# A decode kernel of gated attention and MLP: the MLP's hidden units laid out as 10 full groups, 16 and 80 instead of 9 full groups, 64 and 160

## The chip, the cores and the metric

The kernel runs on one core of one Trainium2 chip. The metric is the device time of one execution in microseconds. One execution reads 78 MB from HBM and writes 1 KB.

## The reference

One token of width 512. Attention has 32 heads of 128 with a cache of 4096 positions per head; the MLP has 1376 hidden units and a squared ReLU. A sigmoid gate mixes the two. All inputs are bf16.

```
x = A_x                                              # 1 x 1 x 512
g = sigmoid((x * gate_w).sum(-1))
q = (x @ wq) as 32 heads of 128
p = softmax(q . k_cache / sqrt(128))                 # 32 x 4096
a = (p @ v_cache) as 4096 @ wo                       # 1 x 1 x 512
h = relu(x @ w1 + b1) ** 2                           # 1376
b = h @ w2 + b2                                      # w2: 1376 x 512
return g * a + (1 - g) * b
```

## The kernel before, in words

All transfers of size are issued by SyncE, one after the other, on one queue of the 16 DMA engines: wq (L243), then the first load of K (load_k(0)), the MLP's weights (L276 to L280), the second load of K, the first of V, and from there K and V in turn, eight loads of each, and at the end wo in four pieces (L291). A load is 128 partitions of 32 KB: four heads, 128 positions on each partition, 32 partitions to a head. Kt holds three loads, Vt two, so a load waits until the buffer that it overwrites has been used up. The MLP's weights lie in the third buffer of K (WM), so load_k(2) waits for the MLP's last matmul (s_ml, L254).

For each of the eight groups of four heads the scores are made on three engines at once. GpSimd multiplies 4 x 17 positions of K by q into pg (L310), and VectorE sums them (psums, L677). VectorE multiplies and sums 2 x 14 positions itself (prods, sums). TensorE transposes the other 32 (L425), ScalarE copies the transposes to kT (L339), and TensorE makes scores of them (L439). VectorE takes maxima, ScalarE the exponentials E (L356), TensorE sums p times V into pO (pv, L470), and after a copy to pvf the heads are picked out into O (extract, L479). At the end the 32 heads are put in order (regroup) and multiplied by wo: attn_rows(c) works through the 32 rows of wo as its four pieces land (16, 8, 6 and 2 rows), and L731 adds the MLP's part.

The MLP is done once, on TensorE, after the first group's scores:

- mlp_h makes h as one row of 1376 on one partition, in T.
- ScalarE copies that row to hrow (L376) and, for 64 of the units, to pvf with every second column left zero, twice (L378).
- mlp_c turns the row into columns: 19 transposes (FN + TX) into H, a column for each row of w2 that a partition holds.
- VectorE applies the squared ReLU and (1 - g) (mlp, L693 and L695), which gives hs.
- mlp_out multiplies each column by its row of w2, 19 matmuls into pO on four rows in turn; ScalarE copies the sum to pvf (L381), and mlp_cols adds its four rows into acc.

How the 1376 units lie on partitions is set by FG, FR, TX and QX. Units 0 to F0 - 1 (FG groups of 128) lie FG to a partition, and the partition's FG rows of w2 are one run of memory (w2a, L277). The next FR = 64 units lie on all 128 partitions as half rows: partition 2u + x holds half x of row u (w2b, L278), so two columns with every second partition zero are needed for them (pvf above), each for 256 of the 512 outputs. The last 160 units lie on QX = 20 partitions, TX = 8 rows of w2 to a partition (WX). WX is loaded by four transfers of five partitions each (L279 and L280): transfer r takes partitions r, r + 4, r + 8, r + 12 and r + 16. The six transfers of w2 count up s_w2, for which mlp_out waits.

SyncE's queue is fed by nothing else; ScalarE issues four small transfers at the start (x, the gate's weights, b1 and b2).

Of the kernel before, what the change touches and what calls it, by code (L numbers as in the profile page):

```python
# [5 lines left out]
def bass_gated_mix__gqa_block_cached__dense_activation_squared_relu__decode_kernel(  # L6
# [18 lines left out]
    ACT = mybir.ActivationFunctionType  # L25
# [7 lines left out]
    DM = 512  # L33
    F = 1376


    FG = 9
    FR = 64
    F0 = FG * 128
    F1 = F0 + FR  # L40
    TX = 8
    QX = 20
    FN = FG + 2
    SCALE = float(D) ** -0.5


# [34 lines left out]
    w1_v = B_w1.rearrange("(p t) n -> p (t n)", t=4)  # L81
    w2_v = B_w2[0:F0, :].rearrange("(p g) n -> p (g n)", g=FG)
    w2_x = B_w2[F1:F, :].rearrange("(q t) n -> q (t n)", t=TX)

    ctx = ExitStack()
    with ctx:
# [9 lines left out]
        Kt = sb("Kt", [128, NK, NB * 128], bf16)  # L96
# [4 lines left out]
        WM = Kt[:, 2, :]  # L101
# [7 lines left out]
        w1_sb = WM[:, 0:4 * F]  # L109
        w1_t = w1_sb.rearrange("p (t n) -> p t n", t=4)  # L110
        w2a = WM[:, 4 * F:4 * F + FG * DM]
        WH = DM // 2
        w2b = WM[:, 4 * F + FG * DM:4 * F + FG * DM + WH]
        WX = Kt[0:QX, 2, 4 * F + FG * DM + WH:4 * F + FG * DM + WH + TX * DM]
        xrow = sb("xrow", [1, DM], bf16)
        grow = sb("grow", [1, DM], bf16)
        b1r = sb("b1r", [1, F], bf16)
# [6 lines left out]
        identf = sb("identf", [128, 128], fp32)  # L124
        pick = sb("pick", [128, 4, 60], fp32)
        pvf = sb("pvf", [112, 512], fp32)
# [14 lines left out]
        omg = sb("omg", [128, 1], fp32)  # L141
        hr = sb("hr", [128, FN + TX], fp32)

        hrow = Vt[0:1, 1, 0:2 * F].bitcast(fp32)
        hs = sb("hs", [128, FN + TX], bf16)
        b2g = sb("b2g", [128, 128], fp32)

        TT = pb("T", [128, NT * 512], fp32)
# [3 lines left out]
        pO = pb("pO", [128, 512], fp32)  # L152
# [7 lines left out]
        SL = pS[0:NH, 0:256].bitcast(bf16)  # L160
        H = pX[:, 160:160 + FN + TX]

# [25 lines left out]
        s_w2 = sem("s_w2")  # L188
# [8 lines left out]
        s_ho = sem("s_ho")  # L197
# [35 lines left out]
        s_hw = sem("s_hw")  # L233
# [10 lines left out]
        with nc.Block() as block:  # L244

            @block.sync
            def _(eng):
                def load_k(i):
                    if i >= NK:
                        eng.wait_ge(s_t, CB[i - NK + 1])  # L250
                        eng.wait_ge(s_mu, XP * (i - NK + 1))
                        eng.wait_ge(s_pm, GP * (i - NK + 1))  # L252
                    if i == 2:
                        eng.wait_ge(s_ml, 1)  # L254
                    eng.dma_start(Kt[:, i % NK, :], k_p[i * 128:(i + 1) * 128, :]).then_inc(s_k[i % NK], 16)

                def load_v(i):
                    if i == 1:
                        eng.wait_ge(s_qr, NQ)
                        eng.wait_ge(s_h, 2)  # L260
                    if i < NQ - 2:
                        if i >= NV:
                            eng.wait_ge(s_pv, i - NV + 1)
                        eng.dma_start(VT(i), v_p[i * 128:(i + 1) * 128, :]).then_inc(s_v[i % NV], 16)
                        return
                    eng.wait_ge(s_t, CB[i])
                    eng.wait_ge(s_mu, XP * i)
                    eng.wait_ge(s_pm, GP * i)
                    if i == NQ - 2:
                        eng.dma_start(VT(i), v_p[i * 128:(i + 1) * 128, :]).then_inc(s_vl[0], 16)  # L270
                    else:
                        for u, a, b in ((1, 0, VG * 512), (2, VG * 512, NG * 512)):
                            eng.dma_start(VT(i)[:, a:b], v_p[i * 128:(i + 1) * 128, a:b]).then_inc(s_vl[u], 16)  # L273

                load_k(0)
                eng.dma_start(w1_sb, w1_v).then_inc(s_w1, 16)  # L276
                eng.dma_start(w2a, w2_v).then_inc(s_w2, 16)  # L277
                eng.dma_start(w2b, B_w2[F0:F1, :].rearrange("u (x n) -> (u x) n", x=2)).then_inc(s_w2, 16)  # L278
                for r in range(4):  # L279
                    eng.dma_start(WX[r:QX:4, :], w2_x[r:QX:4, :]).then_inc(s_w2, 16)  # L280
                load_k(1)
                load_v(0)
                load_k(2)
                for i in range(NQ):
                    if i >= 1:
                        load_v(i)
                    if i + LAG < NQ:
                        load_k(i + LAG)
                eng.wait_ge(s_pv, NQ - 3)
                for c in range(NW):  # L290
                    eng.dma_start(WO[:, TS[c] * DM:TS[c + 1] * DM], wo_v[:, TS[c] * DM:TS[c + 1] * DM])\  # L291
                       .then_inc(s_wo[c], 16)
                eng.wait_ge(s_fin, 1)
                eng.dma_start(out[0, 0, :].rearrange("(j p) -> j p", p=128), b2w[0:128:32, :]).then_inc(s_out, 16)
# [21 lines left out]
            def _(eng):  # L316
# [47 lines left out]
                for i in range(NQ + 1):  # L364
                    if i == NQ:
                        pv_copy(NQ - 3)
                        pv_copy(NQ - 2)
                    if i < NQ:
                        for c in range(NC[i]):
                            evac(CB[i] + c)  # L370
                            if c == 1 and i >= 3:
                                pv_copy(i - 3)
                        score_copy(i)
                        if i == 0:
                            eng.wait_ge(s_h, 1)
                            eng.activation(hrow, TT[0:1, 0:F], ACT.Copy).then_inc(s_hw, 1)  # L376
                            for x in range(2):
                                eng.activation(pvf[0:1, 129 * x:128 + 128 * x:2], TT[0:1, F0:F1], ACT.Copy)\  # L378
                                   .then_inc(s_hw, 1)
                            eng.wait_ge(s_ml, 1)  # L380
                            eng.activation(pvf[:, :], pO[0:112, :], ACT.Copy).then_inc(s_mc, 1)  # L381
                    if i >= 1:
                        neg_max(i - 1)
                        exps(i - 1)

            @block.tensor
            def _(eng):
                eng.wait_ge(s_id, 2)
                for c in range(4):
                    mm = eng.transpose(SL[:, c * 128:c * 128 + 128], ident[:, c:128:4], ident[:, :])  # L390
                mm.then_inc(s_sl, 1)
                eng.wait_ge(s_x, 32)
                for t in range(4):
                    mm = eng.matmul(XC[:, t:t + 1], xrow[:, t:DM:4], ident[0:1, 0:1], start=True, stop=True)
# [11 lines left out]
                for j in range(NQ):  # L406
                    if j >= NT:
                        wait_q(eng, j - NT)
                    for t in range(4):
                        mm = eng.matmul(T[j % NT][:, :], xb[:, t, :], wq_sb[:, t, j * 512:(j + 1) * 512],  # L410
                                        start=(t == 0), stop=(t == 3))
# [76 lines left out]
                def units(n):  # L488
                    if n < FG:
                        return hrow[:, n:F0:FG]  # L490
                    if n < FN:
                        return pvf[0:1, 128 * (n - FG):128 * (n - FG) + 128]
                    return hrow[:, F1 + n - FN:F:TX]

                def mlp_h():
                    eng.wait_ge(s_w1, 16)
# [8 lines left out]
                    mm.then_inc(s_h, 1)  # L505

                def mlp_c():
                    eng.wait_ge(s_hw, 3)
                    eng.wait_ge(s_ho, 10)
                    for n in range(FN + TX):  # L510
                        mm = eng.transpose(H[0:128 if n < FN else QX, n:n + 1], units(n), identf[0:1, 0:1])
                    mm.then_inc(s_h, 1)

                def mlp_out():
                    eng.wait_ge(s_w2, 16 * 6)
                    eng.wait_ge(s_hs, 1)
                    for n in range(FN + TX):
                        c, lhs = slice(0, DM), hs[:, n:n + 1]
                        if n < FG:
                            rhs = w2a[:, n * DM:(n + 1) * DM]  # L520
                        elif n < FN:
                            c = slice(WH * (n - FG), WH * (n - FG) + WH)
                            rhs = w2b
                        else:
                            lhs = hs[0:QX, n:n + 1]
                            rhs = WX[:, (n - FN) * DM:(n - FN + 1) * DM]
                        r = 32 * (n % 4)
                        mm = eng.matmul(pO[r:r + 1, c], lhs, rhs, start=(n < 4), stop=(n >= FN + TX - 4),
                                        skip_group_check=True)
                    mm.then_inc(s_ml, 1)  # L530

                def mlp_cols():
# [75 lines left out]
            def _(eng):  # L608
                eng.memset(b2w[:, :], 0.0).then_inc(s_wm, 1)
                eng.memset(pick[:, :, :], 0.0).then_inc(s_ho, 1)  # L610
                eng.memset(pvf[0:1, 0:256], 0.0).then_inc(s_ho, 1)
                eng.memset(pO[:, :], 0.0).then_inc(s_ho, 1)
                eng.memset(RS[:, :], 0.0).then_inc(s_ho, 1)
                eng.memset(onec[:, :], 1.0).then_inc(s_ho, 1)
                eng.memset(onesf[:, :], 1.0).then_inc(s_ho, 1)
                eng.wait_ge(s_id, 2)
                eng.tensor_copy(identf[:, :], ident[:, :]).then_inc(s_ho, 1)
                eng.wait_ge(s_ho, 7)
                eng.tensor_reduce(pick[:, :, 28:32],
                                  identf[:, :].rearrange("p (c r) -> p c r", c=4)[:, :, 0:16]  # L620
                                  .rearrange("p c (b h) -> p b h c", b=4), AX.X, ALU.add).then_inc(s_ho, 1)
# [139 lines left out]
```

## Time and profile before

| | |
|---|---|
| time, median of 3 runs | 190.63 us (190.62 to 190.68) |
| the profiled execution | 190.78 us |
| its span | 189.3 us |
| mean granted TensorE clock | 0.667 |

The span runs from the first to the last instruction; the profiled execution's own time is 1.5 us longer. Idle time of an engine that is not the bound costs nothing, so the rows of interest are those of the engines and queues that are busy throughout, and the chain of work that ended last: it is followed back from the last instruction, at each step to what released it. The DMA view, given a window, counts the packets that start in it, with their bytes and their time as a share of 16 engines' time in that window; a packet is one partition's row of a transfer, or the 4 bytes with which a DMA engine signs off its part of a transfer. In a window shorter than its packets that share can be over 100%: share x 16 x window / packets is the mean duration of one.

### The profile page before, as it was taken

How to read it: one execution, taken by the hardware profiler on the slowest of the kernel's cores; microseconds unless marked ns; L12 is line 12 of the kernel's file. 1: busy time of each engine (PE TensorE's matmuls, PEld its weight loads, DVE VectorE, ACT ScalarE, POOL GpSimd, SP SyncE). 2: the span in 40 equal slices, each digit the busy share in tenths (PEclk: the TensorE clock that was granted, in tenths of full speed). 3: DMA queues.
4: the chain of work that ended last, by engine and by line, in shares of the span. 5: the costliest groups of instructions: out<-in, count | busy, mean ns of one | idle time of the engine just before them, and what ended most of it. 6: DMA issues, size and time to landing. Idle time of an engine off the chain costs nothing. (4 is left out here: it accounts for less than half of the span.)

```text
span 189.3 us, 2567 instructions
## 1 busy us (share of the span) xinstructions
PE 105.0 (55%) x1049; PEld 62.6 (33%) x1049; DVE 152.7 (81%) x126; ACT 69.6 (37%) x171; POOL 137.8 (73%) x38
## 2 busy tenths in 40 slices
PE   1139867688104838156507381857283758567843
PEld 0113243346104616132404180417140742224222
DVE  5112569999997899999999999999999999990112
ACT  2103485328321729404910573056405551406000
POOL 1000199998996999979998998999899989930000
PEclk9999999555555857658955855556755585555596
DMA  6999999999999999999999999999999999999991
GB/s 222 444 443 443 389 456 432 422 408 443 441 443 422 443 438 433 402 422 422 440 443 443 422 443 433 422 408 429 429 440 443 443 415 443 403 426 410 433 390 50
DMA packets 3672, 78.47 MB, mean 414 GB/s; under 512 B 439, under 2 KB 569, under 8 KB 826
## 3 DMA queue, kind: packets, MB, share of 16 engines
q1 hardware_dynamic: 3648, 78.32, 96.8%
q8 instruction: 8, 0.13, 0.3%
q14 instruction: 2, 0.02, 0.0%
q10 hardware_dynamic: 14, 0.01, 0.0%
HBM read 78.32 MB, written 0.00 MB: 414 GB/s over the span
## 5 line engine op out<-in xcount | busy, mean ns | idle before, releaser
L310 POOL TENSOR_TENSOR pg<-Kt,qb 128x2176 f32<-128x2176 bf16 x32 | 137.1, 4313 | 28.8 <-DMA Kt<-in_A_k_cache_dram 23.3
L677 DVE TENSOR_REDUCE Sb<-pg 128x17 f32<-128x2176 f32 x32 | 77.0, 2405 | 1.8 <-POOL pg L310 1.8
L339 ACT ACTIVATE kT<-T 128x1024 bf16<-128x1024 bf16 x32 | 30.8, 1030 | 17.5 <-PE T L425 17.3
L425 PE MATMUL T<-ident,Kt 128*128 128x128 bf16 x256 | 25.6, 281 | 19.5 <-DMA Kt<-in_A_k_cache_dram 19.5
L662 DVE TENSOR_TENSOR pr<-Kt,pQ 128x1792 f32<-128x1792 bf16 x16 | 32.2, 2011 | 1.9 <-DMA Kt<-in_A_k_cache_dram 1.1
L671 DVE TENSOR_REDUCE Sb<-pr 128x14 f32<-128x1792 f32 x16 | 32.1, 2003 | 0.0
L425 PEld LDWEIGHTS T<-ident,Kt 128*128 128x128 bf16 x256 | 22.3, 130 | 24.1 <-DMA Kt<-in_A_k_cache_dram 22.4
L470 PE MATMUL pO<-Vt,E 128*16 128x512 bf16 x192 | 22.5, 562 | 0.9 <-issue 0.9
L349 ACT ACTIVATE nM<-pM 128x4 f32<-128x4 f32 x8 | 1.4, 173 | 48.1 <-PE pM L453 48.1
L356 ACT ACTIVATE E<-Sb,nM 32x128 bf16<-32x128 f32 x32 | 18.6, 582 | 0.9
L439 PE MATMUL pS<-qc,kT 128*128 128x4 bf16 x256 | 11.8, 168 | 9.7 <-ACT kT L339 9.4
L479 PE MATMUL pX<-pvf,pick 112*32 112x128 f32 x64 | 14.2, 396 | 2.3 <-ACT pvf L362 1.5
L439 PEld LDWEIGHTS pS<-qc,kT 128*128 128x128 bf16 x256 | 10.0, 103 | 11.9 <-ACT kT L339 11.7
L449 PE MATMUL pM<-identf,mp 128*1 128x128 f32 x8 | 2.8, 346 | 19.3 <-DVE mp L684 19.3
L410 PE MATMUL T<-Vt,kT 128*128 128x512 bf16 x32 | 10.7, 482 | 3.3 <-DMA Vt<-in_A_wq_dram 3.3
L479 PEld LDWEIGHTS pX<-pvf,pick 112*32 112x32 f32 x64 | 9.3, 157 | 6.7 <-ACT pvf L362 2.5
L331 ACT ACTIVATE qb<-T 32x128 bf16<-32x128 f32 x20 | 5.4, 268 | 10.3 <-PE T L410 10.0
L453 PE MATMUL pM<-gm,onesf 1*128 1x4 f32 x16 | 4.3, 334 | 8.5 <-DVE gm L688 8.5
L470 PEld LDWEIGHTS pO<-Vt,E 128*16 128x16 bf16 x192 | 6.5, 106 | 7.3 <-issue 5.3
L649 DVE CAST qb<-T 32x128 bf16<-32x128 f32 x12 | 3.4, 287 | 6.5 <-PE T L410 6.2
L470 PE MATMUL pO<-Kt,E 128*16 128x512 bf16 x64 | 7.2, 629 | 2.0 <-issue 2.0
L453 PEld LDWEIGHTS pM<-gm,onesf 1*128 1x128 f32 x16 | 3.6, 276 | 13.9 <-DVE gm L688 13.9
(78 smaller groups left out, 67.4 us busy)
## 6 DMA issues: line engine op xcount, KB each, us to landing
Kt<-in_A_k_cache_dram SPq DMA_DIRECT2D x8, 4096.0 KB, 31.7
Vt<-in_A_v_cache_dram SPq DMA_DIRECT2D x6, 4096.0 KB, 31.6
Vt<-in_A_wq_dram SPq DMA_DIRECT2D x1, 4096.0 KB, 12.2
Kt<-in_A_v_cache_dram SPq DMA_DIRECT2D x1, 4096.0 KB, 35.8
Kt<-in_A_v_cache_dram SPq DMA_DIRECT2D x1, 3072.0 KB, 25.1
Vt<-in_A_wo_dram SPq DMA_DIRECT2D x1, 2048.0 KB, 31.6
Kt<-in_B_w_dram SPq DMA_DIRECT2D x1, 1376.0 KB, 24.4
Kt<-in_B_w_dram SPq DMA_DIRECT2D x1, 1152.0 KB
```

The costliest lines, as they stand in the source:

```text
L310: eng.tensor_tensor(pg[:, n % 2, 0:g, :], Kt[:, i % NK, k * g * 128:(k + 1) * g * 128] .rearrange("p (b d) -> p b d", b=g), qb[:, i:i + 1, ...
L339: eng.activation(kT[:, n % NR, :], T[n % NT][:, :].bitcast(bf16), ACT.Copy).then_inc(s_ev, 1)
L356: eng.activation(E[a:b, j % NE, :, h], Sb[a:b, j % NS, :], ACT.Exp, bias=nM[a:b, 4 * j + h:4 * j + h + 1], scale=SCALE, accum_out=RS[a:b, ...
L410: mm = eng.matmul(T[j % NT][:, :], xb[:, t, :], wq_sb[:, t, j * 512:(j + 1) * 512], start=(t == 0), stop=(t == 3))
L425: mm = eng.transpose(T[n % NT][:, :].bitcast(bf16)[:, y * 128:(y + 1) * 128], Kt[:, i % NK, w * 128:(w + 1) * 128], ident[:, :])
L439: mm = eng.matmul(S[:, c * TC + y, :], kT[:, n % NR, y * 128:(y + 1) * 128], qc[:, 4 * i:4 * i + 4], start=True, stop=True)
L453: eng.matmul(MB[:, 4 * i:4 * i + 4], onesf[:, :], gm[:, 4 * i:4 * i + 4], start=True, stop=True) .then_inc(s_mb, 1)
L470: mm = eng.matmul(pO[r:r + 16, :], E[:, i % NE, 4 * y:4 * y + 4, :], VT(i)[:, y * 512:(y + 1) * 512], start=(y < 4), stop=(y >= NG - 4))
L479: mm = eng.matmul(O, pick[0:112, b, 28 - 4 * i:60 - 4 * i], pvf[:, b * 128:(b + 1) * 128], start=False, stop=(i == NQ - 1 and b == 3), ski ...
L662: eng.tensor_tensor(pr[:, 0:x, :], Kt[:, i % NK, a * 128:(a + x) * 128] .rearrange("p (b d) -> p b d", b=x), PQ[:, i % 4:i % 4 + 1, :].bro ...
L671: eng.tensor_reduce(Sb[:, i % NS, a:a + x], pr[:, 0:x, :], AX.X, ALU.add).then_inc(s_sd, 1)
L677: eng.tensor_reduce(Sb[:, i % NS, k * g:(k + 1) * g], pg[:, n % 2, 0:g, :], AX.X, ALU.add)\
```

## The change

The units lie as 10 full groups (FG = 10), 16 units one to a partition on 16 partitions (FR = 16), and 80 units as four rows of w2 on each of 20 partitions (TX = 4, QX = 20). The bytes of w2 are the same 1376 rows of 1 KB. On all partitions a row of w2a is 10 KB instead of 9; w2b is 16 rows of 1 KB instead of 128 of 512 B; each partition of WX takes 4 KB instead of 8, in the same four transfers of five partitions. The half rows are gone, and with them their fill on VectorE (L611), the two copies on ScalarE (L378) and one column: FN + TX is 15 instead of 19. Two counts of semaphores fall with the instructions that are left out.

```
-    FG = 9
-    FR = 64
+    FG = 10
+    FR = 16
     F0 = FG * 128
     F1 = F0 + FR
-    TX = 8
+    TX = 4
     QX = 20
-    FN = FG + 2
+    FN = FG + 1
...
         w2a = WM[:, 4 * F:4 * F + FG * DM]
-        WH = DM // 2
-        w2b = WM[:, 4 * F + FG * DM:4 * F + FG * DM + WH]
-        WX = Kt[0:QX, 2, 4 * F + FG * DM + WH:4 * F + FG * DM + WH + TX * DM]
+        w2b = Kt[0:FR, 2, 4 * F + FG * DM:4 * F + FN * DM]
+        WX = Kt[0:QX, 2, 4 * F + FN * DM:4 * F + (FN + TX) * DM]
...
-                eng.dma_start(w2b, B_w2[F0:F1, :].rearrange("u (x n) -> (u x) n", x=2)).then_inc(s_w2, 16)
+                eng.dma_start(w2b, B_w2[F0:F1, :]).then_inc(s_w2, 16)
...
-                            for x in range(2):
-                                eng.activation(pvf[0:1, 129 * x:128 + 128 * x:2], TT[0:1, F0:F1], ACT.Copy)\
-                                   .then_inc(s_hw, 1)
...
                 def mlp_c():
-                    eng.wait_ge(s_hw, 3)
-                    eng.wait_ge(s_ho, 10)
+                    eng.wait_ge(s_hw, 1)
+                    eng.wait_ge(s_ho, 9)
                     for n in range(FN + TX):
-                        mm = eng.transpose(H[0:128 if n < FN else QX, n:n + 1], units(n), identf[0:1, 0:1])
+                        mm = eng.transpose(H[0:height(n), n:n + 1], units(n), identf[0:1, 0:1])
...
                     for n in range(FN + TX):
-                        c, lhs = slice(0, DM), hs[:, n:n + 1]
-                        if n < FG:
-                            rhs = w2a[:, n * DM:(n + 1) * DM]
-                        elif n < FN:
-                            c = slice(WH * (n - FG), WH * (n - FG) + WH)
-                            rhs = w2b
+                        if n < FN:
+                            rhs = w2a[:, n * DM:(n + 1) * DM] if n < FG else w2b
                         else:
-                            lhs = hs[0:QX, n:n + 1]
                             rhs = WX[:, (n - FN) * DM:(n - FN + 1) * DM]
                         r = 32 * (n % 4)
-                        mm = eng.matmul(pO[r:r + 1, c], lhs, rhs, start=(n < 4), stop=(n >= FN + TX - 4),
-                                        skip_group_check=True)
+                        mm = eng.matmul(pO[r:r + 1, :], hs[0:height(n), n:n + 1], rhs, start=(n < 4),
+                                        stop=(n >= FN + TX - 4))
...
-                eng.memset(pvf[0:1, 0:256], 0.0).then_inc(s_ho, 1)
```

height(n) is new: 128 for a full group, FR for the column of w2b, QX for those of WX.

More of the change, by code (lines that the diff above doesn't have):

```diff
@@ L490, in units, with height @@
                         return hrow[:, n:F0:FG]
-                    if n < FN:
-                        return pvf[0:1, 128 * (n - FG):128 * (n - FG) + 128]
-                    return hrow[:, F1 + n - FN:F:TX]
+                    return hrow[:, F0:F1] if n == FG else hrow[:, F1 + n - FN:F:TX]
+                def height(n):
+                    return 128 if n < FG else FR if n == FG else QX
                 def mlp_h():
@@ L617, in _ @@
                 eng.tensor_copy(identf[:, :], ident[:, :]).then_inc(s_ho, 1)
-                eng.wait_ge(s_ho, 7)
+                eng.wait_ge(s_ho, 6)
                 eng.tensor_reduce(pick[:, :, 28:32],
```

## The prediction

> **What bounds the kernel now.** I read the page first (sums, slices, queues), then the chain of waits from the end backwards, then the DMA view in narrow windows. From the page, parts 1 to 3:
>
> ```profile
> span 189.3 us, 2567 instructions
> PE 105.0 (55%) x1049; PEld 62.6 (33%) x1049; DVE 152.7 (81%) x126; ACT 69.6 (37%) x171; POOL 137.8 (73%) x38
> DMA  6999999999999999999999999999999999999991
> q1 hardware_dynamic: 3648, 78.32, 96.8%
> q8 instruction: 8, 0.13, 0.3%
> q14 instruction: 2, 0.02, 0.0%
> ```
>
> No compute engine is full, but the 16 DMA engines are, in every slice but the first and the last. The chain of waits (start us, us, what) says the same of the end:
>
> ```profile
> 151.20 35.03 DMA Vt<-in_A_wo_dram
> 186.23 0.04 issue
> 186.27 1.05 PE pX L557 x25
> 187.35 0.29 DVE b2w L731
> ```
>
> The third transfer of wo is issued at 151.20, waits 35.03 us behind a full queue, and 1.4 us after it lands the result is added up. From the timeline of the end:
>
> ```profile
> 184.43 0.09 PEld L551 LDWEIGHTS pO<-Vt,o 128*1 128x1 bf16 x4 [1.86 <-DMA Vt<-in_A_wo_dram]
> ```
>
> TensorE had already waited 1.86 us for the second transfer of wo there: compute has room at the end. So only work that the DMA engines do counts, and, because a transfer is complete when its last engine is done, only the work of the engine that ends last. The table of windows, last stretches (window, length, busy time and instructions of PE, PEld, DVE, ACT, POOL, clock, DMA share, GB/s), and the DMA view of 185.69 to 185.72 (first row) and of 185.72 to 186.39 (second and third):
>
> ```profile
> 185.50:185.75 0.25, 0.13 (x8) 0.10 (x8) 0.06 (x1) 0.00 (x0) 0.00 (x0) 1.00 0.17 66
> 185.75:186.00 0.25, 0.25 (x8) 0.00 (x0) 0.00 (x0) 0.00 (x0) 0.00 (x0) 1.00 0.09 33
> 186.00:186.25 0.25, 0.02 (x3) 0.00 (x0) 0.00 (x0) 0.00 (x0) 0.00 (x0) 0.60 0.06 25
> DMA packets 1, 0.00 MB, mean 0 GB/s; under 512 B 1, under 2 KB 1, under 8 KB 1
> DMA packets 9, 0.02 MB, mean 24 GB/s; under 512 B 1, under 2 KB 1, under 8 KB 9
> q1 hardware_dynamic: 9, 0.02, 6.4%
> ```
>
> A packet under 512 B on this queue is an engine's sign-off of a transfer (4 B). The last other engine signs off at 185.7; from 185.72 to 186.39 the share is 6.4%, one sixteenth: one engine works alone for 0.69 us. Call it E. All others have slack against it.
>
> **Which engine E is.** This decides the sign. The four five-row transfers (L280) run on five engines alone. The DMA view of 28.66 to 29.31, where no other packets start:
>
> ```profile
> DMA packets 22, 0.09 MB, mean 139 GB/s; under 512 B 11, under 2 KB 11, under 8 KB 11
> q1 hardware_dynamic: 22, 0.09, 33.7%
> ```
>
> 11 packets of 8 KB with 11 sign-offs; five engines a third of sixteen busy. All four transfers go to the same five: they stay behind. The next load of K shows it, windows 37.70 to 38.25, 38.25 to 38.90 and 38.90 to 39.75:
>
> ```profile
> DMA packets 24, 0.46 MB, mean 834 GB/s; under 512 B 10, under 2 KB 10, under 8 KB 10
> DMA packets 2, 0.07 MB, mean 101 GB/s; under 512 B 0, under 2 KB 0, under 8 KB 0
> DMA packets 22, 0.52 MB, mean 617 GB/s; under 512 B 6, under 2 KB 6, under 8 KB 6
> ```
>
> Ten sign off, none for 0.65 us, then six: the five, and one that was hit by a fetch of instructions (queue q8) before. The latest of the five starts that load alone at 29.81; a load of 4.19 MB takes 9.7 us; and a fetch of q14 stands at 68.6 to 68.7, followed by one stretched packet. DMA views of 29.805 to 29.82, 77.2 to 86.9, 68.6 to 68.7, 68.96 to 69.30:
>
> ```profile
> q1 hardware_dynamic: 1, 0.03, 505.8%
> DMA packets 144, 4.19 MB, mean 432 GB/s; under 512 B 16, under 2 KB 16, under 8 KB 16
> q14 instruction: 1, 0.01, 20.2%
> q1 hardware_dynamic: 1, 0.03, 34.3%
> ```
>
> 29.81 + 4 x 9.71 = 68.65: the fetch falls on this very engine at the end of its fourth load. It costs it 20.2% x 16 x 0.1 = 0.32 us, and the next 32 KB take 34.3% x 16 x 0.34 = 1.87 us against 505.8% x 16 x 0.015 = 1.21: 0.98 us in all. So E is one of the five, late by the five-row transfers and by one fetch. That the lone engine at 186.4 is this one, I infer from the order of sign-offs, which stays the same from load to load.
>
> **The change part by part, on the DMA engines.** Prices per packet, DMA views of 26.2 to 27.2 (9216 B), 24.0 to 24.9 (11008 B), 28.057 to 28.068 (512 B; four and a sign-off), 184.13 to 184.32 (6144 B), 185.80 to 186.35 (2048 B):
>
> ```profile
> q1 hardware_dynamic: 45, 0.41, 97.6%
> q1 hardware_dynamic: 35, 0.39, 100.4%
> q1 hardware_dynamic: 5, 0.00, 66.5%
> q1 hardware_dynamic: 5, 0.03, 38.7%
> q1 hardware_dynamic: 7, 0.01, 6.7%
> ```
>
> Share x 16 x window / packets gives 0.347, 0.413, 0.027 (with 0.009 off for the sign-off, from 1.9% x 16 x 0.03 in the one-packet row of 185.69, rest by four), 0.235 and 0.084 us. The 8 KB packet: (33.7% x 16 x 0.65 - 11 x 0.009) / 11 = 0.310.
>
> - WX: each of the five engines moves one row of each transfer, 4 x 8 KB now, 4 x 4 KB after, with the same sign-offs. 4 KB was not seen; it lies between 0.084 (2 KB) and 0.235 (6 KB); halfway is 0.160. 4 x (0.310 - 0.160) = 0.60 us less; by the ends 0.30 to 0.90.
> - w2a: every engine still moves eight rows, of 10240 B instead of 9216. Between 0.347 and 0.413 by size, 0.385: 8 x 0.038 = 0.30 us more on all 16; by the ends 0 to 0.53.
> - w2b: 128 rows of 512 B, eight on each engine, become 16 rows of 1 KB. If these spread over all 16, one row each: 8 x 0.027 - 0.046 (1 KB, between 0.027 and 0.084) = 0.17 us less; by the ends 0.13 to 0.19; on five engines, with four rows on some, it would be 0.03.
>
> E: -0.60 + 0.30 - 0.17 = **-0.47 us**. The eleven others: +0.30 - 0.17 = **+0.13 us**. E's lead of 0.69 over the second shrinks to 0.69 - 0.60 = 0.09 if the second is one of the eleven, so E still ends last, by a hair.
>
> [...]
>
> **The compute side**, from the groups of lines between 30 and 42 us, SyncE's waits, and the DMA view of 41.18 to 47.50:
>
> ```profile
> L528 PE MATMUL pO<-Kt,hs 128*1 128x512 bf16 (+2 forms) x19 | 2.4, 587 | 0.8 <-DVE hs L695 0.8
> L511 PE MATMUL pX<-identf,Vt 1*128 1x1 f32 (+1 forms) x17 | 1.5, 207 | 1.6 <-ACT pvf L378 1.6
> L378 ACT ACTIVATE pvf<-T 1x64 f32<-1x64 f32 x2 | 0.3, 202 | 0.0
> SPq L255 <- PE pO L528: 33.9, 1, 33.9
> q1 hardware_dynamic: 80, 2.62, 96.3%
> ```
>
> ScalarE loses two copies (0.3), TensorE four of its 19 transposes (4 x 0.2, at most 0.8) and, of 19 matmuls into pO, three full widths of 18 (2.4 x 3 / 18 = 0.4); VectorE loses one fill at the start, where it later waits anyway. mlp_out thus ends at most 1.5 us earlier, likely 0.4 to 1, as VectorE takes H only when its sum of pg is done. SyncE waits for just this before it issues K's third load, but the queue behind it holds work: from that issue (41.18) to 47.5 the engines are 96.3% busy with loads issued before. I cost it at nothing; if the queue ever ran dry there, the whole 0.4 to 1 us would be gained. SyncE issues the same six weight transfers in the same order, with two full loads queued ahead, and no queue is moved past another. No wait is added: the counts fall with the instructions.
>
> The tail after wo is the same instructions. It may start at full clock instead of half (the clock drops from 1.00 to 0.60 in the window at 186.00): at most 32 matmuls, a quarter of 1.05 us if all ran so; taken as nothing.
>
> **Sum.** Profiled execution 190.78, span 189.3: 190.78 - 0.47 = 190.31. The runs' median is 190.63, 0.15 below the profiled one; on it, 190.16.
>
> **Rivals.**
> 1. E stops being last. The fetch that hits E cost 0.98 because it fell at a load's end. VectorE and ScalarE have one and two instructions less before it, TensorE sixteen, so fetches move in time. If this one is cheaper, E falls behind the second, which sets the floor: gain 0.69 - 0.13 = 0.56, 190.07. For: the hair of 0.09. Against: the fetch waits for a packet's end wherever it comes.
> 2. Small transfers cost by piece, not by byte: then WX gives back nothing, and w2a's 0.30 less w2b's 0.17 lands on E: 190.76, slower. It decides from a 4 KB price of 0.28 up (0.310 - 0.13 / 4). Against: 6 KB at 0.235. [...]
> 3. E is not of the five, my thread of sign-offs being wrong: the same +0.13 on the last engine, 190.76.
> 4. A fetch that has hit another engine falls on one of the five: the 0.98 of the row above on top, 190.63 - 0.47 + 0.98 = 191.14. For: moved fetches. Against: no engine of the five but E is that late at the end.
> 5. It does nothing that can be told: a fetch on one of the eleven grows by 0.3, that engine ends last, gain 0.2, 190.43.
>
> **How the numbers follow.** Forecast 0.62 (its own range 190.0 to 190.35, from the 4 KB price and the start's scatter), rival 1 0.13, 2 0.05, 3 0.06, 4 0.04, 5 0.10. The measurement can tell 0.2%, 0.38 us: faster means below 190.25. The forecast clears it by 0.09, so I give it 0.50 of its 0.62, and rival 1 wholly: faster 0.63. Within: 0.12 of the forecast, rivals 2, 3 and 5, less 0.02 for the chance that 2 or 3 is larger: 0.31. Slower: rival 4 and that 0.02, 0.06. Range 189.95 to 190.55: rival 1 with a quicker tail below; 5 above; 2 to 4 are left out, 0.15, and 0.05 lies below.
>
> **What would show it.** Packets: 20 of 4 KB near 0.16 us at 28 to 29 us; 16 of 1 KB; 128 of 10 KB near 0.385. Six late engines at the end of K's second load still, but by some 0.6 us less than before against the ten. Third wo transfer landing near 185.75, its wait still ending the chain, and the lone engine's stretch cut from 0.69 to some 0.1. Wrong it would be if that stretch stays, if the gap of 0.65 us without sign-offs near 38.5 does not shrink, or if the chain ends in something other than a transfer of wo.

## The result, and the profile after

| | before | after |
|---|---|---|
| median of 21 runs each, side by side | 190.61 us | 190.29 us |
| ratio, 95% interval | | 0.9984 [0.9977, 0.9991] |
| the profiled execution | 190.78 us | 190.35 us |
| its span | 189.3 us | 188.9 us |

The kernel is faster by 0.32 us; by the interval, by 0.17 to 0.44. The page of the kernel after, the lines that answer to those of before:

```profile
span 188.9 us, 2548 instructions
PE 106.4 (56%) x1041; PEld 62.7 (33%) x1041; DVE 152.5 (81%) x125; ACT 69.4 (37%) x169; POOL 137.7 (73%) x38
DMA  6999899999999999999999999999999999999992
q1 hardware_dynamic: 3536, 78.32, 97.2%
```

The bytes are the same and the DMA engines are as full as before. What has changed is who ends last. The DMA view of the kernel after, 185.98 to 186.04 (first row) and 186.04 to 186.10 (second):

```profile
DMA packets 3, 0.00 MB, mean 34 GB/s; under 512 B 2, under 2 KB 2, under 8 KB 3
DMA packets 1, 0.00 MB, mean 0 GB/s; under 512 B 1, under 2 KB 1, under 8 KB 1
```

Two engines sign off their last packet between 185.98 and 186.04, and the last one within 0.1 us of them. The stretch of 0.69 us in which one engine worked alone is gone. The chain of waits of the kernel after (start us, us, what) no longer ends in a transfer:

```profile
181.92 0.20 DVE o L717
182.12 0.04 issue
182.17 1.88 PE pO L543 x16
184.04 0.02 issue
184.07 0.62 PE pO L543 x3
184.69 0.02 issue
184.71 0.70 DVE pvf L719
185.41 0.04 issue
185.46 0.60 PE pX L558 x8
186.06 0.83 PE pX L549 x26
```

In this execution compute set the end: 16 matmuls with wo took 1.88 us. The windows from 182 to 184 us, before and then after, say why they took 1.03 before (granted clock in the column before the DMA share):

```profile
182.00:184.00 2.00, 1.03 (x16) 0.32 (x16) 0.00 (x0) 0.00 (x0) 0.00 (x0) 1.00 0.99 401
```

```profile
182.00:184.00 2.00, 1.83 (x16) 0.38 (x16) 0.11 (x1) 0.00 (x0) 0.00 (x0) 0.50 1.00 411
```

The clock was 1.00 there in the one execution and 0.50 in the other. That is not the change's doing: the kernel before, profiled twice more below, has 0.50 in this window both times, and its 16 matmuls are busy for 1.65 and 1.67 us. In a second profiled execution of the kernel after, the chain ends in the second piece of wo, which lands at 183.97 with 2.9 us of compute behind it:

```profile
150.64 33.33 DMA Vt<-in_A_wo_dram
183.97 0.04 issue
184.02 0.62 PE pO L543 x3
184.64 0.02 issue
184.66 0.70 DVE pvf L719
185.37 0.04 issue
185.41 0.60 PE pX L558 x8
186.02 0.92 PE pX L549 x24
```

So transfers and compute now end within some tenths of each other.

### The profile page after: what moved, and what is told of

The parts are those of the page before. It is cut to its first block, busy times and chain, and to the rows that moved or that the text cites. A ratio compares the mean times of both kernels' runs of the same rounds, so it can differ in the third digit from the quotient of the medians.

```text
span 188.9 us, 2548 instructions
## 1 busy us (share of the span) xinstructions
PE 106.4 (56%) x1041; PEld 62.7 (33%) x1041; DVE 152.5 (81%) x125; ACT 69.4 (37%) x169; POOL 137.7 (73%) x38
## 3 DMA queue, kind: packets, MB, share of 16 engines
q1 hardware_dynamic: 3536, 78.32, 97.2%
HBM read 78.32 MB, written 0.00 MB: 415 GB/s over the span
## 5 line engine op out<-in xcount | busy, mean ns | idle before, releaser
L466 PE MATMUL pO<-Vt,E 128*16 128x512 bf16 x192 | 21.7, 542 | 0.1
L475 PE MATMUL pX<-pvf,pick 112*32 112x128 f32 x64 | 15.3, 419 | 3.1 <-ACT pvf L361 2.4
L475 PEld LDWEIGHTS pX<-pvf,pick 112*32 112x32 f32 x64 | 9.8, 166 | 7.6 <-ACT pvf L361 2.9
L355 ACT ACTIVATION_READ_ACCUMULATOR E<-Sb,nM 32x1 f32 x32 | 8.1, 254 | 0.0
```

The lines of the kernel that those rows point to most:

```text
L355: eng.activation(E[a:b, j % NE, :, h], Sb[a:b, j % NS, :], ACT.Exp, bias=nM[a:b, 4 * j + h:4 * j + h + 1], scale=SCALE, accum_out=RS[a:b, ...
L466: mm = eng.matmul(pO[r:r + 16, :], E[:, i % NE, 4 * y:4 * y + 4, :], VT(i)[:, y * 512:(y + 1) * 512], start=(y < 4), stop=(y >= NG - 4))
L475: mm = eng.matmul(O, pick[0:112, b, 28 - 4 * i:60 - 4 * i], pvf[:, b * 128:(b + 1) * 128], start=False, stop=(i == NQ - 1 and b == 3), ski ...
```

## The experiments

Each was timed beside the kernel before on the same chip, which took 190.53 to 190.61 there; the ratios are against it. The changed kernel stands at 0.9984, and at 0.9985 in the repetition below.

**The kernel before, profiled twice more.** No edit.

> The kernel before, profiled once more. The gain came out at 0.3 where the sum said 0.47 from one profiled execution that took 190.78, 0.2 over the median. Theory (in that execution the last engine's lead was large, since a fetch met the end of a load): here one engine works alone at the end for 0.2 to 0.5 us, not 0.69, and the packet behind its fetch of q14 takes less than 1.87; chain of waits through the second or third transfer of wo. Rival (the lead is the same in every execution, and something else took 0.15 us of the gain): 0.6 to 0.75 alone.

> As the run beside it, for a third execution of the kernel before: the lead again 0.2 to 0.5 by the theory, 0.6 to 0.75 by the rival; between the two executions it differs by the scatter of the first transfers.

The profiled executions took 190.62 and 190.44 us. The DMA view of the first, 185.99 to 186.01 and 186.14 to 186.17:

```profile
DMA packets 2, 0.00 MB, mean 103 GB/s; under 512 B 1, under 2 KB 1, under 8 KB 2
DMA packets 1, 0.00 MB, mean 0 GB/s; under 512 B 1, under 2 KB 1, under 8 KB 1
```

The second-last sign-off is at 186.00 and the last at 186.15: alone for 0.15 us; in the third execution (185.98 to 186.01 and 186.16 to 186.19, one sign-off each) for 0.17 to 0.20. The rival is out, and the lead is even below the theory's 0.2 to 0.5: the 0.69 on which the prediction was built belonged to that one execution, the longest of the three. Its last engine ended at 186.4 and these at 186.15 to 186.2. The cause that the theory gave is not it, though. The packet behind the fetch of q14 takes no less than before; DMA view of the first of the two, 68.695 to 68.705:

```profile
q1 hardware_dynamic: 1, 0.03, 1166.9%
```

Share x 16 x 0.01 is 1.87 us, and the third execution has the same row at 68.71 to 68.72. What differs between the executions is told further down.

**The changed kernel once more.** No edit.

> The changed kernel itself, for a comparison in one call with the next three. 190.2 to 190.4, 0.2 to 0.4 under before; the five engines of the five-row transfers sign off K's second load 0.6 us closer to the ten than before; its chain of waits ends in the second or third transfer of wo, or, where the clock is halved at the end, in compute.

190.25 us, 0.9985 [0.9976, 0.9994]. The gain stands in the repetition.

**The five-row transfers doubled.**

```
+        WY = Kt[0:QX, 2, 4 * F + (FN + TX) * DM:4 * F + (FN + 2 * TX) * DM]
...
+                for r in range(4):
+                    eng.dma_start(WY[r:QX:4, :], w2_x[r:QX:4, :]).then_inc(s_w2, 16)
...
-                    eng.wait_ge(s_w2, 16 * 6)
+                    eng.wait_ge(s_w2, 16 * 10)
```

> The changed kernel, with four more transfers of five rows of 4 KB into columns that nothing reads; the MLP waits for them too. Compute is that of the changed kernel to the instruction. Theory: the same five engines get 4 x (0.160 + 0.009) = 0.68 us more, the eleven nothing; the last of the five ends 0.6 to 0.7 later than in the changed kernel and sets the end: 190.8 to 191.0, 0.2 to 0.4 over before. Rival (compute brings the gain): that of the changed kernel, 190.2 to 190.4. [...]

190.69 us, 1.0010 [1.0001, 1.0018]: about 0.45 more than the changed kernel, and slower than before. With compute unchanged, 80 KB on five engines take the whole gain back, so the gain is the five engines' and not the MLP's. The time lies below the theory's 190.8 to 191.0, since 0.45 is 0.2 less than the 0.68 that the five were given; that fits a changed kernel whose end is not set by the five alone.

**The MLP made longer.**

```
-                    for n in range(FN + TX):
+                    for n in list(range(FN + TX)) * 2:
                         mm = eng.transpose(H[0:height(n), n:n + 1], units(n), identf[0:1, 0:1])
```

> The changed kernel with its 15 transposes done twice, the same values into the same columns: the MLP ends some 1.5 us later and the load of K behind it is issued so much later. Theory: the queue has over 6 us of work there, so the time is that of the changed kernel, 190.2 to 190.4 (0.1 more at most by shifted fetches of instructions, since TensorE has 30 more). Rival (the MLP's compute is on the path): 1 us or more longer, 191.3 and up.

190.41 us, 0.9996 [0.9987, 1.0005]. SyncE's timeline, the changed kernel and then this one:

```profile
41.30 0.80 SPq L254 DMA_DIRECT2D Kt<-in_A_k_cache_dram  x2
```

```profile
42.96 0.81 SPq L254 DMA_DIRECT2D Kt<-in_A_k_cache_dram  x2
```

The load behind the MLP is issued 1.66 us later, and by the ratios the time is 0.2 more, with intervals that overlap. The MLP is hidden; whether it costs that 0.2 can't be told.

**The compute part alone.** Against the changed kernel:

```
-    FG = 10
-    FR = 16
+    FG = 9
+    FR = 64
...
-    TX = 4
+    TX = 8
```

> The compute part alone: 9 full groups, 64 units one to a partition on 64 partitions (whole rows of 1 KB instead of half rows of 512 B on 128), WX of before with eight rows on 20 partitions. The two copies, the fill, one transpose and one half-width pair of matmuls are gone as in the change; w2a and WX move the same bytes as before. Theory (the DMA engine that ends last sets the time): w2b is four rows of 1 KB on each engine, 4 x 0.046 = 0.18 us, against 8 x 0.027 = 0.22: 0.03 less, so 190.5 to 190.65, no change against before; five engines stay late by 1.3 us after the weights. Rival (the MLP's shorter compute brings the gain): the time of the changed kernel, 190.2 to 190.35.

190.78 us, 1.0017 [1.0008, 1.0026]: not the rival's 190.2 to 190.35, but the theory missed too. Some 0.2 us over the time of before came from somewhere, and while that is open this run alone can't say what the compute part is worth. In the trace the next load's first packets take 1.44 to 1.56 us instead of 1.21 on the eleven engines without five-row transfers, right after the 64 rows of 1 KB.

**64 more rows, on adjacent and on alternate partitions.** These two ask what the 64 rows did:

```
+                eng.dma_start(Kt[0:64, 2, 4 * F + (FN + TX) * DM:4 * F + (FN + TX + 1) * DM], B_w2[0:64, :]).then_inc(s_w2, 16)
...
-                    eng.wait_ge(s_w2, 16 * 6)
+                    eng.wait_ge(s_w2, 16 * 7)
```

and the same with Kt[0:128:2].

> The changed kernel with one more transfer, 64 rows of 1 KB onto partitions 0 to 63, into columns that nothing reads; it asks how whole rows on 64 partitions came to cost 0.3 us more than half rows on 128. Every engine moves four more packets of 0.046: 0.18 us. Theory (what is written onto half of the partitions backs up, and the next packets wait): the first 32 KB packets of the next load take about 0.3 us longer than 1.21, as they did with 64 rows in the run of the compute part alone; 190.6 to 190.9. Rival (packets of 1 KB cost by number alone): those packets take 1.21 to 1.25, 190.4 to 190.6.

> The same 64 rows onto every second partition of 128, all else equal. [...] Rival (it is the source, 64 KB of one run of memory, or the number of packets): as with adjacent partitions.

190.79 us, 1.0013 [1.0005, 1.0022], on adjacent partitions; 190.54, 0.9997 [0.9988, 1.0005], on alternate ones. One 32 KB packet of the next load, DMA view of 28.85 to 28.86 (adjacent) and of 28.92 to 28.93 (alternate):

```profile
q1 hardware_dynamic: 1, 0.03, 909.4%
```

```profile
q1 hardware_dynamic: 1, 0.03, 778.1%
```

Share x 16 x 0.01 is 1.46 and 1.25 us; one in the kernel before, at 28.44, took 758.1%, 1.21. With adjacent partitions 1.46 is the least of the eleven engines, most of which take 1.54; 1.25 is what the changed kernel has without these rows. The five engines are slowed one step earlier, in their packets of 4 KB: one at 28.88 with adjacent partitions, then one at 28.87 with alternate ones (DMA views of 28.875 to 28.885 and of 28.865 to 28.870):

```profile
q1 hardware_dynamic: 1, 0.00, 185.0%
```

```profile
q1 hardware_dynamic: 1, 0.00, 198.8%
```

That is 0.30 us in the first window, of 0.01 us, and 0.16 in the second, of 0.005. The same rows from the same memory cost 0.25 us more on one half of the partitions. It is where they are written.

**No five-row transfers at all.** FR = 96, TX = 0: the last 96 units one to a partition.

```
-    FR = 16
+    FR = 96
...
-    TX = 4
+    TX = 0
...
-                for r in range(4):
-                    eng.dma_start(WX[r:QX:4, :], w2_x[r:QX:4, :]).then_inc(s_w2, 16)
...
-                    eng.wait_ge(s_w2, 16 * 6)
+                    eng.wait_ge(s_w2, 16 * 2)
```

> 10 full groups and the other 96 units one to a partition on 96 partitions: w2b is 96 rows of 1 KB, six on each of 16 engines, and there is no WX: four issues, four transposes and four matmuls fewer than in the changed kernel. Theory: against the changed kernel the five engines lose 0.68 and all get 5 x 0.046 = 0.23, so the five are 0.45 earlier, the eleven 0.23 later. The eleven that had a fetch of instructions end within 0.1 to 0.3 of the last one in the changed kernel and now are last: 190.35 to 190.55, not better than the changed kernel. Rival (fewer and evener transfers and less compute are always better): 189.9 to 190.2.

190.83 us, 1.0017 [1.0008, 1.0026]. "Fewer and evener" is out. It is 0.3 over the theory's upper end, and rows on 96 adjacent partitions slow the packets behind them nearly as on 64 (the next load's first packets take 1.37 to 1.46 us), so it says less on the eleven than it was meant to.

**The 80 units as one transfer over all engines.**

```
-    TX = 4
-    QX = 20
+    TX = 5
+    QX = 16
...
-                for r in range(4):
-                    eng.dma_start(WX[r:QX:4, :], w2_x[r:QX:4, :]).then_inc(s_w2, 16)
+                eng.dma_start(WX, w2_x).then_inc(s_w2, 16)
...
-                    eng.wait_ge(s_w2, 16 * 6)
+                    eng.wait_ge(s_w2, 16 * 3)
```

> The changed kernel with its 80 last units as five rows on each of 16 partitions, in one transfer: every one of the 16 engines moves 5 KB there, about 0.20 us, instead of 4 x 0.17 on five. It is the run without five-row transfers once more, without the many rows of 1 KB that backed up there. Theory (the last engine sets the end; in the changed kernel the five and those of the eleven that had a fetch end within 0.1 to 0.2 us): the five gain 0.48, the eleven lose 0.20 and end last, 190.35 to 190.5, no better than the changed kernel. Rival (even transfers are better): 189.8 to 190.1.

191.46 us, 1.0048 [1.0035, 1.0061]: 0.9 over before and 1 us over the theory. 80 KB go onto 16 adjacent partitions, and the packet that follows (28.78 to 28.79) takes 1109.4% x 16 x 0.01 = 1.78 us:

```profile
q1 hardware_dynamic: 1, 0.03, 1109.4%
```

Against 1.21 that is some 0.6 us lost, and the first packets of all sixteen engines take 1.51 to 1.87. That the eleven end last once the five-row transfers are gone could not be shown apart from this by either run; it stays an inference there, though in one execution of the changed kernel itself one of them does, as told below.

**Only the first piece of wo.** This kernel leaves out the last 16 of a partition's 32 rows of wo: they aren't loaded, and what lies there is multiplied.

```
-                for c in range(NW):
+                for c in range(1):
                     eng.dma_start(WO[:, TS[c] * DM:TS[c + 1] * DM], wo_v[:, TS[c] * DM:TS[c + 1] * DM])\
...
-                    eng.wait_ge(s_wo[c], 16)
+                    if c < 1:
+                        eng.wait_ge(s_wo[c], 16)
```

> The changed kernel, which loads only the first of the four pieces of wo; the last 16 of a partition's 32 rows of wo are left out of the transfers and whatever lies there is multiplied. The DMA engines end 5 us earlier and nothing after the first piece waits for them, so the time is that of the compute chain. Theory as predicted (compute has room at the end, 1.9 us by the wait of TensorE before): over 1 us less, 189.2 or under. Rival (the compute chain is close behind the transfers, and hides what more the transfers would give): at most 0.3 less, 189.9 to 190.3. The chain of waits then reaches back through the exponentials to VectorE's sums, and where its last matmuls run at half clock they take twice as long.

189.21 us, 0.9933 [0.9909, 0.9956], but from 187.75 to 190.04 in nine runs. The runs fall into two groups, one near each theory: four runs at 189.76 to 190.04, with a mean clock of 0.64 to 0.66, and five at 187.75 to 189.21, with 0.68 to 0.72. The timeline of the profiled one (190.04) shows 20 matmuls in 2.3 us:

```profile
182.00 2.30 PE L544 MATMUL pO<-Vt,o 128*1 128x512 bf16 x20 [0.28 <-DVE o L718]
```

With transfers out of the way, the end is where the clock puts it: 0.2 us under the changed kernel, or 2.5.

**The second piece of wo split.**

```
-    TS = [0, 16, 24, 30, 32]
+    TS = [0, 16, 20, 24, 30, 32]
```

> The changed kernel with wo in five pieces: the second, of 8 rows, split into 4 and 4, so that the 20 rows that the wide sum takes are in some 0.6 us earlier. The chain of waits of most runs so far ends in that second piece: four matmuls, the copy to pvf, the wide rows, the last 32 matmuls, 2.9 us in all. Theory (that wait is the one that ends last, and the piece behind it lands 0.1 to 0.2 us short of mattering): 0.1 to 0.2 less than the changed kernel, 190.05 to 190.2, and the chain then ends in the piece before the last. Rival (compute at half clock or that later piece holds the end): 190.2 to 190.4.

190.45 us, 0.9992 [0.9983, 1.0001]: no better than the changed kernel, so the theory's 0.1 to 0.2 did not come. The chain of waits now ends as it did before the change, in the piece of wo that ends at row 30, with 1.05 us behind it:

```profile
185.89 0.04 issue
185.93 1.05 PE pX L549 x32
```

The wait moved from one piece to the next, and nothing was won.

## Why the prediction was right, and where it was not

- **What bounds.** Right for the kernel before, whose chain of waits ends in a transfer of wo in all three profiled executions (the third, the second and the fourth piece); of two executions of the changed kernel one does, and the other ends in compute, which the prediction had named as a sign against itself. Doubling the five engines' bytes moved the time; lengthening the MLP by 1.66 us did not.
- **The five-row transfers.** Right, with its price. One packet of 4 KB in the kernel after (28.26 to 28.27), then 38 of 10 KB (27.0 to 28.0), then one of 1 KB (28.21 to 28.22):

```profile
q1 hardware_dynamic: 1, 0.00, 99.4%
q1 hardware_dynamic: 38, 0.39, 91.4%
q1 hardware_dynamic: 1, 0.00, 28.8%
```

  0.159, 0.385 and 0.046 us, against 0.160, 0.385 and 0.046 in the sum. The rival of costs by the piece falls with the first of them: behind a full queue, halving the four transfers from 40 to 20 KB halved the time of their packets, from 0.310 to 0.159 us. The 0.17 for w2b took it that its 16 rows go to all 16 engines, one each, which no run had shown; in the kernel after, 16 packets of 1 KB start between 28.20 and 28.83 (53 packets under 2 KB there, 37 of them sign-offs), each as a sign-off ends and none as another of them ends, so they do. The five stay behind by less: from 38.60 to 38.90 four engines sign off, three of them of the five, where the kernel before has a gap without sign-offs from 38.25 to 38.90:

```profile
DMA packets 10, 0.20 MB, mean 655 GB/s; under 512 B 4, under 2 KB 4, under 8 KB 4
```
- **The size of the gain.** 0.47 in the sum, 0.32 measured, which is less than the 0.38 that the prediction took for the least that can be told; the interval from 21 runs each tells it. The step that was mis-sized is "one engine works alone for 0.69 us", from which the prediction took it that E still ends last: in two more executions of the kernel before it was 0.15 and 0.17 to 0.20.
- **Who ends last.** In these traces an engine starts its next packet some 4 ns before its last one ends (before: a packet of 32 KB ends at 29.342, the next starts at 29.338), so the packets can be followed engine by engine, which the prediction left to inference. E is what it was taken for: in all three executions before, the last engine is one of the five, hit by the fetch of q14 near 68.5. It began K's second load at 29.81 in the first and at 29.55 and 29.56 in the others, which is half of the difference in lead. But the eleven have a cost that the prediction did not price: in each execution fetches of q8 hit eight of them, and seven end 1.5 to 1.6 us later for it, against 0.97 for E and its fetch. Before, the five began that load 1.17 to 1.34 us after the eleven on average, and with 0.97 more one of them ended last. After, it is 0.47 and 0.60 in two executions, and 0.53 + 0.97 against 1.55 is level: in one the last engine is one of the eleven (186.08, the latest of the five 185.73), in the other one of the five (186.00, against 185.93). The eleven also began that load some 0.3 later than before, where the sum had 0.13 for them. So the floor that rival 1 names was reached, without a cheaper fetch. What part of the rest is compute's cannot be told from these runs.
- **The room of compute.** Wrong as stated. The 1.86 us in which TensorE waited for wo were read as room, but the clock was full there, and behind that same wait come matmuls, copy and wide rows that lead to the end, 2.9 us in the second execution of the changed kernel. At half clock TensorE's wait there is 0.39 us in that execution and none in the first. The sum did not rest on it, as the second and the third piece move together; what rested on it is the tail "taken as nothing".
- **The MLP's compute.** Hidden, as said, but not shorter by 0.4 to 1 us: from the groups of lines, after,

```profile
L520 PE MATMUL pO<-Kt,hs 128*1 128x512 bf16 (+2 forms) x15 | 2.4, 606 | 1.1 <-DVE hs L686 1.1
```

  the 15 matmuls are as long as the 19 were (2.4 us busy), and SyncE's load is issued at 41.30, not before 41.18.
- **Rivals 2, 3 and 4** (cost by the piece, last engine not of the five, a fetch on one of the five) would all have been slower than before, which the interval excludes. E is one of the five in the traces, against rival 3, and no fetch beyond the two of q14 hits one of the five, against rival 4. Rival 5's 0.2 lies inside the interval, and one of the eleven does end last in one execution; but the fetches of q8 cost the eleven no more after than before.

## What to carry to other kernels

When all DMA engines are full, as here (96.8% of their time before), the sum of bytes tells little, since it was 78.32 MB before and after: ask which engine ends last, what it alone was given, and by how much it is later than the engines that the change does not relieve, because no more than that can be won. Count what every engine is given, fetches of instructions too, and take the lead from several executions, since one profile held it some four times too large (0.69 us against 0.15 to 0.20). And before a wait on a transfer is read as room for compute, follow what comes behind it to the end, at the lower of the clocks that the profiles show (0.50 here).

## What the runs showed of the hardware

In these runs, rows written onto few partitions cost more than their packets show. Most of the packets of 1 KB themselves still take 0.046 us, and the bill comes with the packets that follow. The next ones of 32 KB take 1.21 us after 64 rows laid as halves on all 128 partitions, up to 1.25 in the changed kernel and with 64 rows more on every second partition, 1.46 to 1.68 on eleven engines with 64 adjacent ones, and mostly 1.73 to 1.87 after 80 KB on 16. Why the place of the rows counts was not shown.

Fetches of instructions, eight of 16 KB on q8 and two of 8 KB on q14 in an execution (page: 8, 0.13 MB, and 2, 0.02 MB), hold up the engines of the loads. In the profiled executions of the result, before and after, each fetch starts 3 to 5 ns before a packet of q1 ends. One in the kernel before, DMA view of 32.06 to 32.075:

```profile
q8 instruction: 1, 0.02, 461.2%
```

461.2% x 16 x 0.015 = 1.1 us of one engine's time. The packet of 32 KB that starts as the fetch ends takes 1.68 us instead of 1.21; behind seven of the eight fetches of q8 it takes 1.68 to 1.76, before and after. With this packet, a fetch of q8 has made its engine 1.5 to 1.6 us late at the end of the kernel, against the engines without a fetch, and the fetch of q14 that the prediction follows 0.97. With the queue full throughout, none of these engines made that good by the end.
